# Normalising softmax rows inside the transpose, and two small steps moved to ScalarE

## The chip, the cores and the metric

The kernel runs on one core of a Trainium2 chip. The metric is the device time of one execution in microseconds, as the median of several. The core has five engines with a queue each: TensorE (PE, its weight loads PEld), VectorE (DVE), ScalarE (ACT), GpSimd (POOL) and SyncE (SP), which issues the DMAs. Each takes its own instructions in order.

## The reference

Three layers follow each other: an attention that keeps only the 32 largest scores of each row, a mixture of eight experts with all tokens going to all experts, and a feed-forward layer.

```python
scores = scale * q @ k.T                       # 2 batches, 8 heads, 576 positions, head size 64
kth = np.partition(scores, -32, axis=-1)[..., -32:-31]
scores = np.where(scores >= kth, scores, -1e9)
attn = np.exp(scores - scores.max(-1, keepdims=True))
attn = attn / (attn.sum(-1, keepdims=True) + 1e-9)
x = (attn @ v) as (1152, 512)
P = exp(x @ w_gate - max), 8 rounds of row and column normalisation
x = sum over e of P[:, e] * (relu(x @ w1[e]) @ w2[e])     # 512 -> 1024 -> 512, 8 experts
h = x @ w_in;  out = (h * tanh(softplus(h))) @ w_out      # 512 -> 2048 -> 512
```

## The kernel before

The 1152 tokens are nine tiles of 128. The experts go over them in three chunks: tiles 0 and 1, tiles 2 and 3, tiles 4 to 8. First the attention of tiles 0 and 1 runs alone (16 units, one for each tile and head); then the experts of the first two chunks run on TensorE with the attention of tiles 2 to 8 woven in between, then the third chunk, then the feed-forward layer.

A unit of attention is five stages, and `attention()` writes out by hand in which step each unit's stage is issued: step u issues the scores of unit u, the threshold of unit u-2, the mask of unit u-3, the normalisation of unit u-4 (u-3 from unit 13 on) and the values of unit u-5 (u-4). In the steps from 5 on, two further sets of scores (`early`) are made ahead for later tiles and evicted by ScalarE (L239).

- `scores` (L226, L235): products in PSUM, evicted by ScalarE to `s`, 128x576.
- `threshold` (L254, L261): VectorE finds the 32 largest of each row, by four MAX8 of eight each and three MATCH_REPLACE8 between them.
- `exponential` (L271, L272): `nb` is the row's largest score times -0.125, a 128x1 TENSOR_SCALAR on VectorE, and is the bias of ScalarE's exponential.
- `mask`: for the first 13 units (`on_pool`) VectorE makes a mask (L285), GpSimd adds it to the scores (L286), and ScalarE takes the exponential with the sum `sm` beside it. For the others the exponential is taken first, and VectorE masks and sums in one instruction (L290).
- `norm`: VectorE adds epsilon (L299) and takes the reciprocal (L300), and ScalarE multiplies `em`, 128x576, by it in place (L305).
- `values`: TensorE transposes four blocks of 128x128 (L325) with the identity, ScalarE evicts them (L328); for each pair of heads the last 64 columns of both are one further block (L336, L339). Then the products with v (L348, L355), and for tile 1 the two parts of x (L362, L363).

The order on TensorE is the order in which the program issues its work. On the other engines a planner orders the instructions ahead of time, by the streams that the code names with `st(...)`: "first" goes before "evict", "prep" (the weight copies L520 and L522), "attn", "moe" and "fill". Epsilon and reciprocal of the first 13 units are in the stream "moe", the rest of the attention in "attn". The first MAX8 of tile 2 is tied behind the last reciprocal of tile 1 (`live["ends"]`). Of the small tiles (`top`, `nb`, `sm`, `r`) there are four buffers each. The experts' matmuls are L619 (h, whose two parts are made at L537 and L538) and L596 (y); the first chunk's y are spilled through the two buffers `ysp`.

Of the kernel before, what the change touches and what calls it, by code (L numbers as in the profile page):

```python
# [10 lines left out]
F32 = mybir.dt.float32  # L11
F32R = mybir.dt.float32r
U32 = mybir.dt.uint32
AF = mybir.ActivationFunctionType
ALU = mybir.AluOpType
# [4 lines left out]
P = 128  # L20
B, H, S, D = 2, 8, 576, 64
# [4 lines left out]
DM = H * D  # L26
# [8 lines left out]
TOPK = 32  # L35
NEG = -3.0e38
SCALE = 0.125
EPS = 1e-9
TINY2 = ((1 + 1 / 16) * 2.0**-15) ** 2

CHUNKS = [(0, 1), (2, 3), (4, 5, 6, 7, 8)]
# [32 lines left out]
def attention_moe_moe2(ctx: ExitStack, tc: tile.TileContext, qT, kT, vm, vt, wg, wst, w64, out):  # L74
    nc = tc.nc
# [5 lines left out]
    def after(inst, earlier):  # L81

        tc.add_manual_dep(
            inst.ins,
            earlier.ins.name,
            mybir.DependencyInfo(mybir.DependencyClass.NoSync, mybir.DependencyReason.DATA),
            reason="order",
        )

    def pool(name, bufs=1, space=None, stack=ctx, side="left", **kw):  # L90
        if space is not None:
            kw["space"] = space
        return stack.enter_context(tc.tile_pool(name=name, bufs=bufs, side=side, **kw))

    const = pool("const")
    small = pool("small", 4)
    yp = pool("yp", 2)
# [12 lines left out]
    sp = pool("sp", 2, stack=att)  # L110
    hp = pool("hp", LAG + 1, stack=att)

    with st("attn"):
        ident = const.tile([P, P], F32, name="ident")
# [31 lines left out]
    qset, live, away = {}, {}, {}  # L146
# [14 lines left out]
    def load_v(b, pair):  # L161
        hs = slice(2 * pair, 2 * pair + 2)
        m = vp.tile([P, 2, 4, D], F32, tag="vm", name=f"vm_{b}_{pair}")
        nc.sync.dma_start(m, vm[b, :, hs])
        e = vp.tile([P, P], F32, tag="vt", name=f"vt_{b}_{pair}")
        nc.gpsimd.memset(e, 0.0)
        for i in range(2):
            nc.sync.dma_start(e[i * D : (i + 1) * D, i * D : (i + 1) * D], vt[b, :, 2 * pair + i])
        vmain[b, pair], vtail[b, pair] = m, e
# [22 lines left out]
    def queries(t, g):  # L192
        if (t, g) not in qset:
            qset[t, g] = load_q(t, g)
        return qset[t, g]
# [49 lines left out]
    def threshold(t, h, on_pool):  # L245

        with st("attn"):
            s = live["s", t, h]
            top = small.tile([P, TOPK], F32, tag="top", name=f"top_{t}_{h}")
            w = sp.tile([P, S], F32, tag="w", name=f"w_{t}_{h}")  # L250
            src = s
            for i in range(TOPK // 8):
                g = top[:, 8 * i : 8 * i + 8]
                top8 = nc.vector.max(g, src)  # L254
                if i == 0 and t == CHUNKS[0][-1] + 1:
                    if "ends" in live:
                        after(top8, live["ends"])
                    else:
                        live.setdefault("held", []).append(top8)
                if i + 1 < TOPK // 8:  # L260
                    nc.vector.match_replace(w, g, src, NEG)  # L261
                    src = w
            live["top", t, h] = top
            if not on_pool:
                live["e", t, h] = exponential(t, h, sp.tile([P, S], F32, tag="e", name=f"e_{t}_{h}"), s, nc.vector)
        yield from ()

    def exponential(t, h, dst, src, eng, **kw):

        nb = small.tile([P, 1], F32, tag="nb", name=f"nb_{t}_{h}")  # L270
        eng.tensor_scalar(nb, live["top", t, h][:, 0:1], -SCALE, None, op0=ALU.mult)  # L271
        nc.scalar.activation(dst, src, AF.Exp, bias=nb, scale=SCALE, **kw)  # L272
        return dst

    def mask(t, h, on_pool):

        with st("attn"):
            s = live.pop(("s", t, h))
            sm = small.tile([P, 1], F32, tag="sm", name=f"sm_{t}_{h}")
            kth = live["top", t, h][:, TOPK - 1 : TOPK]  # L280
            if h % 2 == 0:
                live["pair", t, h] = sp.tile([P, 2 * S], F32, tag="em", name=f"em_{t}_{h}", bufs=3)
            em = live["pair", t, h - h % 2][:, h % 2 * S :][:, :S]
            if on_pool:
                nc.vector.tensor_scalar(em, s, kth, NEG, op0=ALU.is_lt, op1=ALU.mult)  # L285
                nc.gpsimd.tensor_tensor(em, em, s, ALU.add)  # L286
                exponential(t, h, em, em, nc.vector, accum_out=sm)
            else:
                e = live.pop(("e", t, h))
                nc.vector.scalar_tensor_tensor(em, s, kth, e, op0=ALU.is_ge, op1=ALU.mult, accum_out=sm)  # L290
            live["em", t, h], live["sm", t, h] = em, sm
        yield from ()

    def norm(t, h, on_pool):
        with st("attn"):
            em, sm = live["em", t, h], live.pop(("sm", t, h))
            r = small.tile([P, 1], F32, tag="r", name=f"r_{t}_{h}")
            with st("moe" if on_pool else "attn"):
                nc.vector.tensor_scalar(r, sm, EPS, None, op0=ALU.add)  # L299
                inv = nc.vector.reciprocal(r, r)  # L300
            if (t, h) == (CHUNKS[0][-1], H - 1):
                live["ends"] = inv
                for inst in live.pop("held", ()):
                    after(inst, inv)
            nc.scalar.activation(em, em, AF.Copy, scale=r)  # L305
        yield from ()

    def turned(t, i, name):

        if t <= CHUNKS[0][-1] and i % 2:  # L310
            bank = ps_m.tile([P, 512], F32, tag="mm2", name=name, bufs=2)
        else:
            bank = ps_a.tile([P, 512], F32, tag="tr", name=name)
        return bank.rearrange("p (c k) -> p c k", k=P)

    def values(t, h):

        if "gate" in live:
            yield from gate_logits(*live.pop("gate"))
        j = h % 2  # L320
        with st("attn"):
            em = live.pop(("em", t, h))
            tr = turned(t, h, f"tr_{t}_{h}")
            for c in range(4):
                nc.tensor.transpose(tr[:, c, :], em[:, j * D + c * P :][:, :P], ident)  # L325
            at = sp.tile([P, 4, P], F32, tag="at", name=f"at_{t}_{h}", bufs=2)
            with st("evict"):
                nc.scalar.activation(at, tr, AF.Copy)  # L328
            live["at", j] = at
        yield  # L330
        if j == 0:
            return
        pair = h // 2
        with st("attn"):
            tr2 = turned(t, 1, f"tr2_{t}_{h}")
            nc.tensor.transpose(tr2[:, 0, :], live.pop(("pair", t, h - 1))[:, 4 * P : 5 * P], ident)  # L336
            at2 = sp.tile([P, P], F32, tag="at2", name=f"at2_{t}_{h}")
            with st("evict"):
                nc.scalar.activation(at2, tr2[:, 0, :], AF.Copy)  # L339
        yield  # L340
        with st("attn"):
            if pair == 0:
                live["pv"] = ps_a.tile([P, NC, P], F32, tag="pv", name=f"pv_{t}")
            pv = live["pv"]
            for b, c0, c1, _, _ in queries(t, h // HG):
                for c in range(4):
                    for i in range(2):
                        nc.tensor.matmul(  # L348
                            pv[i * D : (i + 1) * D, pair, c0:c1],
                            vmain[b, pair][:, i, c, :],  # L350
                            live["at", i][:, c, c0:c1],
                            start=(c == 0),
                            stop=False,
                        )
                nc.tensor.matmul(pv[:, pair, c0:c1], vtail[b, pair], at2[:, c0:c1], start=False, stop=True)  # L355
            if t == 4 and pair + 1 < NC:
                load_v(1, pair + 1)
            ci, i = place[t]
            if t == CHUNKS[0][-1]:
                with st("first"):  # L360
                    hi, lo = (x[:, pair, i * P : (i + 1) * P] for x in x_tiles(ci))
                    nc.scalar.activation(hi, pv[:, pair, :], AF.Copy)  # L362
                    nc.vector.tensor_sub(lo, pv[:, pair, :], hi)  # L363
            elif h == H - 1:
                hi, lo = (x[:, :, i * P : (i + 1) * P] for x in x_tiles(ci))
                nc.scalar.activation(hi, pv, AF.Copy)
                nc.vector.tensor_sub(lo, pv, hi)
            if h == H - 1:
                if t == CHUNKS[ci][-1]:
                    live["gate"] = (ci,)  # L370
                live["done"] = t
        yield
# [487 lines left out]
```

## Time and profile before

| | |
|---|---|
| median of 3 runs | 1221.68 us (1221.15 to 1223.91) |
| the profiled execution | 1221.39 us, span 1219.6 us |
| TensorE busy | 1168.7 us, 96% |
| VectorE busy | 854.7 us, 70% |
| ScalarE busy | 660.2 us, 54% |
| GpSimd busy | 540.8 us, 44% |
| the chain that ended last | PE 86%, DVE 11%, DMA 1%, ACT 1% |

The span is the time from the first to the last instruction in the profile; the execution's own time has about 1.8 us around it. Busy shares are means over all stages, so they are read by windows: a table of the busy time of each engine in a stretch. The chain of waits goes from the last instruction back to whatever released each step. In a timeline, an instruction's duration can reach over the start of the next one on the same engine, so the time that it takes from a full queue is read from start to start. Several equal instructions in a row are one line with a count.

### The profile page before, as it was taken

To read this page: it belongs to the slowest core of one execution; us is meant where nothing else is said; L and a number is where in the kernel's file an instruction comes from. 1 tells how busy PE (TensorE), PEld (TensorE's weight loads), DVE (VectorE), ACT (ScalarE), POOL (GpSimd) and SP (SyncE) were. 2 spreads that over 40 slices of the span, in tenths; PEclk is the share of its full clock that TensorE was granted. 3 is DMA by queue.
4 is the path that set the end of the run, shared out by engine and by line. 5 is a ranking of instruction groups with operands and counts; after the bars stand their busy time and mean duration, and the time that the engine had idled before them with its cause. 6 is when DMAs were issued, how large, how long until landed. Compare 5 with 4: busy or idle time off the path is not lost.

```text
span 1219.6 us, 21194 instructions
## 1 busy us (share of the span) xinstructions
PE 1168.7 (96%) x7459; PEld 1048.4 (86%) x7459; DVE 854.7 (70%) x1873; ACT 660.2 (54%) x1321; POOL 540.8 (44%) x424
## 2 busy tenths in 40 slices
PE   2677999999999999999999999999999999999998
PEld 2566888998989899899999999999999999999997
DVE  7999999999999999713656868677666633433221
ACT  6786777877777778654223333333333334554432
POOL 7844778877777877774112112121121122221210
PEclk9899999999999999999999999999999999999999
DMA  8434565576655555665235665656445332223201
GB/s 258 126 129 152 171 178 170 170 224 188 211 163 168 157 162 164 186 220 169 70 89 180 199 190 176 207 178 192 138 134 160 119 98 64 93 95 114 78 26 44
DMA packets 105114, 183.20 MB, mean 150 GB/s; under 512 B 14128, under 2 KB 24624, under 8 KB 105008
## 3 DMA queue, kind: packets, MB, share of 16 engines
q1 hardware_dynamic: 103712, 180.68, 47.6%
q8 instruction: 58, 0.95, 0.3%
q10 hardware_dynamic: 1296, 1.18, 0.3%
q14 instruction: 48, 0.39, 0.1%
HBM read 158.55 MB, written 23.27 MB: 149 GB/s over the span
## 4 chain that ended last, share of the span: by engine, by line
PE 86%; DVE 11%; DMA 1%; ACT 1%; issue 0%; POOL 0%; SPq 0%; POOLq 0%; ACTq 0%
PE h_c2e L619 18%; PE y_c2e L596 18%; PE h_d L619 8%; PE y_d L596 8%; PE y_c0e L596 7%; PE h_c0e L619 7%; PE h_c1e L619 6%; PE y_c1e L596 6%; DVE top L254 4%; DVE w L261 4%; PE pv L348 2%; PE tr L325 2%; PE sc L226 2%; PE pv L355 1%; DVE em L290 1%; DMA wraw_c0e<-in_wst_dram 1%
## 5 line engine op out<-in xcount | busy, mean ns | idle before, releaser
L522 POOL TENSOR_TENSOR wl_c2e<-wraw_c2e,wh_c2e 128x512 fp32r<-128x512 f32 x64 | 84.2, 1315 | 341.2 <-ACT wh_c2e L520 326.5
L522 POOL TENSOR_TENSOR wl_c0e<-wraw_c0e,wh_c0e 128x512 fp32r<-128x512 f32 x128 | 171.6, 1356 | 53.1 <-ACT wh_c0e L520 50.9
L522 POOL TENSOR_TENSOR wl_c1e<-wraw_c1e,wh_c1e 128x512 fp32r<-128x512 f32 x128 | 173.3, 1371 | 48.6 <-ACT wh_c1e L520 45.2
L520 ACT ACTIVATE wh_c2e<-wraw_c2e 128x512 fp32r<-128x512 f32 x128 | 80.8, 632 | 186.9 <-PE y_c2e L596 95.0
L254 DVE MAX8 top<-w 128x8 f32<-128x576 f32 x216 | 157.8, 747 | 0.8
L619 PE MATMUL h_c2e<-xh,wh_c2e 128*128 128x256 f32 (+1 forms) x512 | 158.3, 309 | 0.0
L619 PE MATMUL h_c2e<-xl,wh_c2e 128*128 128x256 f32 (+1 forms) x512 | 158.0, 309 | 0.0
L619 PE MATMUL h_c2e<-xh,wl_c2e 128*128 128x256 f32 (+1 forms) x512 | 157.8, 308 | 0.0
L538 DVE SCALAR_TENSOR_TENSOR hl_c2e<-h_c2e,hh_c2e 128x256 fp32r<-128x256 f32 (+1 forms) x128 | 62.5, 488 | 99.7 <-ACT hh_c2e L537 99.3
L596 PE MATMUL y_c2e<-wh_c2e,hh_c2e 128*128 128x512 f32 x320 | 126.0, 394 | 0.0
L596 PE MATMUL y_c2e<-wl_c2e,hh_c2e 128*128 128x512 f32 x320 | 125.9, 394 | 0.0
L596 PE MATMUL y_c2e<-wh_c2e,hl_c2e 128*128 128x512 f32 x320 | 125.2, 391 | 0.0
L522 POOL TENSOR_TENSOR wl_d<-wraw_d,wh_d 128x512 fp32r<-128x512 f32 x32 | 41.5, 1297 | 160.2 <-ACT wh_d L520 160.2
L520 ACT ACTIVATE wh_c0e<-wraw_c0e 128x512 fp32r<-128x512 f32 x128 | 80.5, 629 | 52.9 <-PE y_c0e L596 21.0
L261 DVE MATCH_REPLACE8 w<-top,w 128x576 f32<-128x576 f32 x144 | 106.4, 740 | 0.0
L557 DVE TENSOR_TENSOR hl_d<-mg_d,hh_d 128x256 fp32r<-128x256 f32 x64 | 38.5, 602 | 91.7 <-ACT hh_d L556 91.7
L520 ACT ACTIVATE wh_c1e<-wraw_c1e 128x512 fp32r<-128x512 f32 x128 | 80.3, 629 | 40.4 <-PE y_c1e L596 16.4
L619 PEld LDWEIGHTS h_c2e<-xh,wh_c2e 128*128 128x128 f32 x512 | 96.2, 188 | 2.5
L619 PEld LDWEIGHTS h_c2e<-xl,wh_c2e 128*128 128x128 f32 x512 | 96.1, 188 | 2.3
L619 PEld LDWEIGHTS h_c2e<-xh,wl_c2e 128*128 128x128 f32 x512 | 96.8, 189 | 0.0
L226 PE MATMUL sc<-ks,q 128*128 128x288 f32 x320 | 63.1, 330 | 26.0 <-ACT early L239 8.2
L537 ACT ACTIVATE hh_c2e<-h_c2e 128x256 fp32r<-128x256 f32 (+1 forms) x128 | 54.8, 428 | 55.3 <-PE h_c2e L619 53.0
(170 smaller groups left out, 3352.8 us busy)
## 6 DMA issues: line engine op xcount, KB each, us to landing
wraw_c0e<-in_wst_dram SPq DMA_DIRECT2D x128, 256.0 KB, 3.0
wraw_c1e<-in_wst_dram SPq DMA_DIRECT2D x128, 256.0 KB, 3.0
wraw_c2e<-in_wst_dram SPq DMA_DIRECT2D x128, 256.0 KB, 3.0
cx<-in_w_dram SPq DMA_DIRECT2D x32, 512.0 KB, 4.2
wraw_d<-w SPq DMA_DIRECT2D x64, 256.0 KB, 2.6
yd<-ysp SPq DMA_DIRECT2D x32, 256.0 KB, 3.6
yb<-yd SPq DMA_DIRECT2D x32, 256.0 KB, 3.2
w<-cc SPq DMA_DIRECT2D x32, 256.0 KB, 3.5
```

The lines of the kernel that those rows point to most:

```text
L226: nc.tensor.matmul(halves[half], q[:, h % HG, :], ks[b, h][:, half * HS : (half + 1) * HS], start=(i == 0), stop=(i == len(terms) - 1),)
L254: top8 = nc.vector.max(g, src)
L261: nc.vector.match_replace(w, g, src, NEG)
L325: nc.tensor.transpose(tr[:, c, :], em[:, j * D + c * P :][:, :P], ident)
L348: nc.tensor.matmul(pv[i * D : (i + 1) * D, pair, c0:c1], vmain[b, pair][:, i, c, :], live["at", i][:, c, c0:c1], start=(c == 0), stop=False,)
L520: nc.scalar.activation(hi, raw, AF.Copy)
L522: eng.tensor_sub(lo, raw, hi)
L537: nc.scalar.activation(h, ps, AF.Relu)
L538: live["hl"] = nc.vector.scalar_tensor_tensor(l, ps, 0.0, h, op0=ALU.max, op1=ALU.subtract)
L557: nc.vector.tensor_sub(l, g, h)
L596: nc.tensor.matmul(y, h[:, j * P : (j + 1) * P], w, start=(f == 0 and k == 0), stop=(f == nf - 1 and k == 2),)
L619: nc.tensor.matmul(ps, w[:, c * P : (c + 1) * P], x[:, c, c0 : c0 + m], start=(k == 0), stop=(k == 3 * NC - 1),)
```

## The change

For tiles 0 and 1 the exponentials are no longer scaled in place. ScalarE multiplies the identity (128x128) by the reciprocals instead, which gives a diagonal, and TensorE multiplies each block of exponentials by it, where it transposed with the identity. The output is the transposed and scaled block. The last block of a pair, which holds 64 columns of either head, becomes two matmuls with 64 columns each, one for each head's diagonal. The diagonals of a pair lie in a tile of `ysp`. Also for tiles 0 and 1, `nb` is made by ScalarE, and for the first 13 units epsilon is added by ScalarE. `top`, `nb` and `sm` get six buffers.

```diff
-            top = small.tile([P, TOPK], F32, tag="top", name=f"top_{t}_{h}")
+            top = small.tile([P, TOPK], F32, tag="top", name=f"top_{t}_{h}", bufs=6)
...
-        nb = small.tile([P, 1], F32, tag="nb", name=f"nb_{t}_{h}")
-        eng.tensor_scalar(nb, live["top", t, h][:, 0:1], -SCALE, None, op0=ALU.mult)
+        nb = small.tile([P, 1], F32, tag="nb", name=f"nb_{t}_{h}", bufs=6)
+        top = live["top", t, h][:, 0:1]
+        if t <= CHUNKS[0][-1]:
+            nc.scalar.activation(nb, top, AF.Copy, scale=-SCALE)
+        else:
+            nc.vector.tensor_scalar(nb, top, -SCALE, None, op0=ALU.mult)
         nc.scalar.activation(dst, src, AF.Exp, bias=nb, scale=SCALE, **kw)
...
-            sm = small.tile([P, 1], F32, tag="sm", name=f"sm_{t}_{h}")
+            sm = small.tile([P, 1], F32, tag="sm", name=f"sm_{t}_{h}", bufs=6)
...
             with st("moe" if on_pool else "attn"):
-                nc.vector.tensor_scalar(r, sm, EPS, None, op0=ALU.add)
+                if on_pool:
+                    nc.scalar.activation(r, sm, AF.Copy, bias=EPS)
+                else:
+                    nc.vector.tensor_scalar(r, sm, EPS, None, op0=ALU.add)
                 inv = nc.vector.reciprocal(r, r)
...
-            nc.scalar.activation(em, em, AF.Copy, scale=r)
+            if t > CHUNKS[0][-1]:
+                nc.scalar.activation(em, em, AF.Copy, scale=r)
+            else:
+                if h % 2 == 0:
+                    live["turn", t, h] = yp.tile([P, DM], F32, tag="ysp", name=f"turn_{t}_{h}")
+                turn = live["turn", t, h - h % 2][:, h % 2 * P :][:, :P]
+                nc.scalar.activation(turn, ident, AF.Copy, scale=r)
...
             for c in range(4):
-                nc.tensor.transpose(tr[:, c, :], em[:, j * D + c * P :][:, :P], ident)
+                part = em[:, j * D + c * P :][:, :P]
+                if t > CHUNKS[0][-1]:
+                    nc.tensor.transpose(tr[:, c, :], part, ident)
+                else:
+                    nc.tensor.matmul(tr[:, c, :], part, live["turn", t, h - j][:, j * P :][:, :P], start=True, stop=True)
...
-            nc.tensor.transpose(tr2[:, 0, :], live.pop(("pair", t, h - 1))[:, 4 * P : 5 * P], ident)
+            tail = live.pop(("pair", t, h - 1))[:, 4 * P : 5 * P]
+            if t > CHUNKS[0][-1]:
+                nc.tensor.transpose(tr2[:, 0, :], tail, ident)
+            else:
+                turn = live.pop(("turn", t, h - 1))
+                for i in range(2):
+                    keys = slice(i * D, (i + 1) * D)
+                    nc.tensor.matmul(tr2[keys, 0, :], tail[:, keys], turn[:, i * P :][:, :P], start=True, stop=True)
```

## Rows read from the trace of the kernel before

**Rows 1.** Windows: busy us of PE, PEld, DVE, ACT, POOL; clock, DMA share, GB/s.

```profile
33.00:104.50 71.50, 51.29 (x321) 40.81 (x321) 71.43 (x181) 58.58 (x136) 41.66 (x34) 0.90 0.45 144
...
108.20:122.20 14.00, 11.93 (x80) 10.44 (x79) 14.00 (x34) 8.76 (x18) 8.81 (x7) 1.00 0.32 94
122.20:1219.60 1097.40, 1092.90 (x7005) 987.70 (x7005) 741.32 (x1599) 570.19 (x1128) 465.44 (x351) 1.00 0.48 148
```

**Rows 2.** Chain that ended last, 95 to 125 us: start, us, what.

```profile
104.47 0.16 DVE r L300
...
121.89 0.33 DVE hl_c0e L538
...
122.27 1.65 PE h_c0e L619 x12
```

**Rows 3.** Groups, VectorE, 0 to 104.5 us: count, busy us, mean ns, idle before.

```profile
L285 DVE TENSOR_SCALAR em<-s,top 128x576 f32<-128x576 f32 x13 | 10.9, 842 | 0.0
...
L299 DVE TENSOR_SCALAR r<-sm 128x1 f32<-128x1 f32 x16 | 2.2, 140 | 0.0
L271 DVE TENSOR_SCALAR nb<-top 128x1 f32<-128x1 f32 x16 | 2.2, 143 | 1.2 <-ACT em L272 1.2
```

**Rows 4.** Timeline, VectorE, 10 to 62 us: start us, us, operation, count, idle before.

```profile
17.57 0.76 DVE L254 MAX8 top<-s 128x8 f32<-128x576 f32 x1 [0.50 <-ACT s L235]
...
25.62 0.15 DVE L271 TENSOR_SCALAR nb<-top 128x1 f32<-128x1 f32 x1 [0.85 <-ACT em L272]
...
25.75 0.80 DVE L285 TENSOR_SCALAR em<-s,top 128x576 f32<-128x576 f32 x1
...
38.27 0.74 DVE L254 MAX8 top<-s 128x8 f32<-128x576 f32 x1
...
44.51 0.74 DVE L261 MATCH_REPLACE8 w<-top,s 128x576 f32<-128x576 f32 x1
...
48.61 1.72 DVE L285 TENSOR_SCALAR em<-s,top 128x576 f32<-128x576 f32 x1
...
55.39 0.50 DVE L285 TENSOR_SCALAR em<-s,top 128x576 f32<-128x576 f32 x1
...
57.26 0.14 DVE L299 TENSOR_SCALAR r<-sm 128x1 f32<-128x1 f32 x1
57.32 0.07 DVE L261 MATCH_VALUE_LOAD w<-top,w 128x8 f32 x1
```

**Rows 5.** Timeline, ScalarE, 20 to 105 us.

```profile
25.40 0.19 ACT L272 ACTIVATION_READ_ACCUMULATOR em<-em,nb 128x1 f32 x1
25.49 1.13 ACT L520 ACTIVATE wh_c0e<-wraw_c0e 128x512 fp32r<-128x512 f32 x2
...
97.36 0.76 ACT L305 ACTIVATE em<-em,r 128x576 f32<-128x576 f32 x1
98.02 0.25 ACT L362 ACTIVATE xh<-pv 128x128 fp32r<-128x128 f32 x1
98.18 0.71 ACT L239 ACTIVATE early<-sc 128x288 f32<-128x288 f32 x2
```

**Rows 6.** Timeline, TensorE, 20 to 77 us.

```profile
30.05 1.12 PE L325 MATMUL tr<-ident,em 128*128 128x128 f32 x4 [8.44 <-ACT em L305]
...
73.82 0.60 PE L325 MATMUL tr<-ident,em 128*128 128x128 f32 x4
74.25 0.27 PE L336 MATMUL tr<-ident,em 128*128 128x128 f32 x1
...
75.21 1.09 PE L348 MATMUL pv<-at,vm 128*64 128x128 f32 x14 [0.32 <-ACT at L328]
76.23 0.49 PE L355 MATMUL pv<-at,vt 128*128 128x128 f32 x2
76.47 0.78 PE L226 MATMUL sc<-ks,q 128*128 128x288 f32 x4
```

**Rows 7.** Waits to 130 us: waiter, awaited, us in total, times, longest.

```profile
PE tr L325 <- ACT em L305: 15.0, 6, 8.4
```

More of the change, by code (lines that the diff above doesn't have):

```diff
@@ L264, in threshold, with exponential @@
             if not on_pool:
-                live["e", t, h] = exponential(t, h, sp.tile([P, S], F32, tag="e", name=f"e_{t}_{h}"), s, nc.vector)
+                live["e", t, h] = exponential(t, h, sp.tile([P, S], F32, tag="e", name=f"e_{t}_{h}"), s)
         yield from ()
-    def exponential(t, h, dst, src, eng, **kw):
-        nb = small.tile([P, 1], F32, tag="nb", name=f"nb_{t}_{h}")
-        eng.tensor_scalar(nb, live["top", t, h][:, 0:1], -SCALE, None, op0=ALU.mult)
+    def exponential(t, h, dst, src, **kw):
+        nb = small.tile([P, 1], F32, tag="nb", name=f"nb_{t}_{h}", bufs=6)
[4 more added lines that the diff above has]
+            nc.vector.tensor_scalar(nb, top, -SCALE, None, op0=ALU.mult)
         nc.scalar.activation(dst, src, AF.Exp, bias=nb, scale=SCALE, **kw)
@@ L286, in mask @@
                 nc.gpsimd.tensor_tensor(em, em, s, ALU.add)
-                exponential(t, h, em, em, nc.vector, accum_out=sm)
+                exponential(t, h, em, em, accum_out=sm)
             else:
```

## The prediction

> **What bounds the kernel now.** I read the windows first. The program is two stretches. From 122.2 us to the end TensorE is busy 1092.9 of 1097.4 us [rows 1]: it has no idle time to give back, and the change adds and removes nothing there. What can move is the moment at which this stretch begins. In 33.0 to 104.5 us VectorE is busy 71.43 of 71.50 us, while TensorE has 51.3 and ScalarE 58.6 of it [rows 1]. The chain of waits says the same: back from 122.27, where TensorE's unbroken work starts, it stays on VectorE, by the h pieces' low part at 121.89 and by the reciprocal at 104.47 [rows 2]. That reciprocal is the last of tiles 0 and 1. Tile 2's first MAX8 is ordered behind it, so VectorE's work up to it is a fixed set: less work there ends the first phase sooner, by as much, if VectorE stays without gaps. TensorE waits 15.0 us on the scaling of em up to 130 us [rows 7], mostly early (8.44 us in one piece at 30.05, rows 6), but VectorE had other units to work on meanwhile, so this wait is not what sets the end.
>
> **The change part by part.**
>
> *VectorE loses 29 small instructions.* 16 bias products (L271) and 13 of the 16 additions of epsilon (L299; units 13 to 15 keep theirs) [rows 3]. Each lasts 0.14 us, but the next instruction starts 0.06 us later (57.26 to 57.32, rows 4); in a full queue the spacing is the price. VectorE waits for scores for the last time at 17.57 [rows 4]; the bias products of units 0 to 2 lie about there or before and give nothing. So 26 x 0.06 = 1.6 us; bounds 1.6 and, by the durations, 29 x 0.14 = 4.1. I take 1.6, since the queue's spacing was seen directly.
>
> *Two stalls in front of L271.* It waited 1.2 us in all for ScalarE's exponential [rows 3], 0.85 us of it at 25.62 [rows 4]: a bias buffer (4 of them) is free only when the exponential four units back has read it. Off VectorE and with 6 buffers that wait is not VectorE's. The next thing in its queue but the epsilon, which also leaves, is the mask at 25.75 [rows 4], which needs neither. I take the whole 1.2; the other end is 0, if the reciprocal, which still needs the sum, is put in the same place and waits there instead.
>
> *The mask L285.* 13 of them take 10.9 us, 0.84 on average [rows 3], between 0.50 (at 55.39) and 1.72 (at 48.61) [rows 4]; 13 x 0.50 would be 6.5. The 4.4 us over that depend on what else runs beside each, and the new order will deal them out anew. I take 0, with 2 us to either side.
>
> *ScalarE: scaling 128x576 becomes 128x128.* The old one takes 0.66 us of the queue (97.36 to 98.02), the nearest 128x128 row 0.16 (98.02 to 98.18) [rows 5]: 16 x 0.50 = 8.0 us less. Added are 29 one-column activations. The nearest row is the accumulator read, 0.19 long with the next start 0.09 later [rows 5]; so 2.6 to 5.5 us more, and I take 0.09, the queue's spacing. Net 5.4 us less (2.5 at least), on an engine that is not the bound. [...]
>
> *New waits on ScalarE.* Each bias product now waits there for the unit's first MAX8. Queued behind it are exponentials, evictions of scores (L235) and of transposes (L328); TensorE and VectorE's next MAX8 wait for these. With 5.4 us less work on it, and idle 12.9 of 71.5 us, I cost this at nothing; without that cover each microsecond by which VectorE is behind ScalarE's order would be lost to evictions. The epsilon follows its exponential on the same engine, at the lowest of the orders in use there (the stream "moe"); see the rivals. The reciprocal no longer sits behind an epsilon on VectorE.
>
> *TensorE: transposes become fp32 matmuls.* Four transposes take 0.43 us of the queue (73.82 to 74.25). A matmul of the same shape, L355, is two records and takes 0.24 (76.23 to 76.47) [rows 6]; four of them 0.96, so 0.53 us more for each unit, 8.5 us for 16. The pair's tail was one transpose, 0.11 at a quarter of 0.43; it becomes two half-width matmuls, four records at 0.073 (75.21 to 76.23 for 14), 0.29: 0.2 more, 1.5 us for 8. That is 10 us at full clock. At 30.05 four transposes span 1.12 us instead of 0.60 [rows 6]; where it is so, the surplus may be double, too. TensorE has 20.2 us idle in 33.0 to 104.5 alone [rows 1], so this lies beside VectorE's work. The rows of L325 and L355 differ by 2.2 times. [...]
>
> *The end of the phase.* After the last reciprocal: scaling, four transposes, eviction, products, first h piece. The scaling gets 0.50 shorter, the transposes 0.53 longer; the tail lies beside the eviction. I take 0, from -0.5 to +0.9.
>
> *Buffers.* top, nb and sm with 6 buffers, and the diagonal in ysp's two buffers, which nothing else uses before the first y is spilled, cost no time of their own.
>
> Sum: 1.6 + 1.2 = 2.8 us less. The profiled execution took 1221.39 us (span 1219.6 and 1.8 around it): 1218.6. The median of before is 0.3 above that execution, so 1218.9 for the median.
>
> **The rivals.**
>
> *The loop gets shorter as well.* With epsilon beside its exponential, the reciprocal has one VectorE slot to wait for instead of two, diagonals and so TensorE's evictions come sooner, and fewer masks are stretched. For it: TensorE's 15.0 us of waiting on em [rows 7], the 4.4 us over in L285. Against: VectorE has no idle time to fill after 33 us. If half of the 4.4 and 1 us of the end are added: 1218.9 - 3.2 = 1215.7.
>
> *The saving is taken back.* Reciprocals are now the place where VectorE waits for ScalarE, which is busy 82% of the phase [rows 1]. If the 1.2 us stay and the slots (1.6) go into such waits or into masks stretched again: 1221.7, no change. The same holds if the time saved before 104.47 is lost among the MAX8s of tile 2, beside which VectorE is busy 14.0 of 14.0 us up to 122.2 [rows 1]. Against: before, the epsilon waited for the same exponential, and after 33 us VectorE stood still for none of them.
>
> *Slower: the epsilon comes late.* A unit's scores are issued on TensorE behind the transposes of an earlier unit, so whatever delays the diagonal delays scores. On ScalarE the epsilon has the lowest order: after the first exponential weight copies follow at once (25.49, rows 5), and in the phase ScalarE is busy 82% of the time. VectorE's reserve is about 6.2 us: unit 6's scores are first read at 38.27 and its first replacement starts only at 44.51 [rows 4], older units filling the time. From 6.2 us of delay in sum VectorE idles, and each further microsecond is lost. An epsilon later by 1 us than VectorE's was, in each of 13 units, gives 13 - 6.2 = 6.8 lost, less the 2.8 gained: 1225.7. Against: ScalarE has 12.9 us of gaps in the phase, one for nearly each epsilon, and on VectorE the epsilon and the reciprocal each had to find a slot in a full queue.
>
> [...]
>
> **How the numbers follow.** A measurement of this kernel tells about 0.2% (2.4 us) from no change, so faster is below 1219.2. Forecast, 1217 to 1220.5: 0.47, of which 0.33 lies below 1219.2. Shorter loop, 1213 to 1217: 0.15. Taken back, 1220.5 to 1224: 0.19. Slower, above 1224: 0.19 (0.13 by a late epsilon, 0.06 by dearer matmuls). Faster 0.48, same 0.33, slower 0.19. The range of 8 in 10 leaves out the lower half of the second case and the upper two thirds of the last: 1214.5 to 1225.0.
>
> **What would show it.** Right: no idle time before L271's successors on VectorE near 25 us, the last reciprocal of tile 1 some 2.8 us earlier than 104.47, TensorE's unbroken work from about 119.5, and the same 1097 us behind it. [...] Wrong: waits of reciprocals on ScalarE, of MAX8 on scores, masks that add up to far from 10.9 us, or TensorE waiting in the stretch behind.

## The result, and the profile after

The changed kernel takes 1230.57 us (median of 4 runs, 1229.88 to 1232.17) beside 1222.8 us of the kernel before in the same runs: 1.0066 times as long, 95% interval 1.0046 to 1.0085. It is slower by about 8 us where 2.8 us less were forecast, and it lies outside the range. The profiled execution took 1232.17 us, its span 1230.2; against the profiled execution of before the span is 10.6 us longer.

Lines moved by the change: the mask is now L289, the reciprocal L307, the diagonal L318, the transposing matmuls L342 and L360, eviction of transposes L345, products L372 and L379, the parts of x L386 and L387, y L620 and h L643.

Windows of after: busy us of PE, PEld, DVE, ACT, POOL; clock, DMA share, GB/s. They answer to [rows 1]; the middle one runs from the last reciprocal of tile 1 to the first h piece.

```profile
33.00:104.50 71.50, 52.69 (x365) 46.06 (x366) 67.84 (x151) 54.77 (x153) 41.69 (x34) 0.86 0.44 139
107.03:110.84 3.81, 3.34 (x34) 2.61 (x33) 3.81 (x8) 1.65 (x4) 0.00 (x0) 1.00 0.18 67
110.80:1230.20 1119.40, 1112.85 (x7085) 999.79 (x7084) 759.75 (x1634) 579.92 (x1145) 471.74 (x357) 1.00 0.47 147
```

The same last stretch of before, which also starts with its first h piece:

```profile
108.20:1219.60 1111.40, 1104.83 (x7085) 998.14 (x7084) 755.32 (x1631) 578.96 (x1145) 474.26 (x357) 1.00 0.47 148
```

Two things are to be seen. First, VectorE is no longer full in the first phase: 67.84 busy of 71.50 where it had 71.43 [rows 1]. Second, and larger: after the first h piece TensorE runs the same 7085 matmuls at the same granted clock, 1.00, and is busy 8.0 us longer (1112.85 against 1104.83). Its idle time is the same 6.6 us in both. So the matmuls themselves have become slower, in a stretch which the change does not touch.

The chain of waits of after (start, us, what), for [rows 2]:

```profile
106.51 0.29 ACT xh L386
106.82 0.29 DVE xl L387
107.11 0.07 DVE r L307
107.19 3.94 DVE top L254 x6
```

The last reciprocal of tile 1 starts at 107.03 instead of 104.47, so the first phase is 2.6 us longer, not 2.8 shorter. The other 8.0 us of the 10.6 are the slower matmuls.

Groups of VectorE in after, 0 to 107.1 us (count, busy us, mean ns, idle before and what ended it), for [rows 3]:

```profile
L254 DVE MAX8 top<-s 128x8 f32<-128x576 f32 x16 | 12.0, 752 | 6.1 <-ACT s L235 6.0
L289 DVE TENSOR_SCALAR em<-s,top 128x576 f32<-128x576 f32 x13 | 9.3, 715 | 0.0
L307 DVE RECIPROCAL r<-r 128x1 f32<-128x1 f32 x16 | 2.4, 151 | 0.6 <-ACT r L304 0.6
L387 DVE TENSOR_TENSOR xl<-pv,xh 128x128 fp32r<-128x128 f32 x3 | 0.9, 288 | 2.3 <-ACT xh L386 2.3
```

And its timeline (start us, us, operation, count, idle before), for [rows 4]:

```profile
23.42 0.76 DVE L254 MAX8 top<-s 128x8 f32<-128x576 f32 x1 [1.71 <-ACT s L235]
...
25.48 0.15 DVE L307 RECIPROCAL r<-r 128x1 f32<-128x1 f32 x1
25.55 0.92 DVE L289 TENSOR_SCALAR em<-s,top 128x576 f32<-128x576 f32 x1
...
106.82 0.29 DVE L387 TENSOR_TENSOR xl<-pv,xh 128x128 fp32r<-128x128 f32 x1 [1.05 <-ACT xh L386]
107.03 0.15 DVE L307 RECIPROCAL r<-r 128x1 f32<-128x1 f32 x1
107.10 1.40 DVE L254 MAX8 top<-early 128x8 f32<-128x576 f32 x2
108.42 2.72 DVE L254 MAX8 top<-early_xh 128x8 f32<-128x576 f32 x4
```

The stall before the bias product (0.85 us at 25.62, rows 4) is gone, but two microseconds earlier the first MAX8 of a unit stands 1.71 us for its scores. At the end the last reciprocal, which has its inputs, is queued behind a low part of x that waits 1.05 us for ScalarE. Behind it six MAX8 of tile 2 run at once, where there were four.

### The profile page after: what moved, and what is told of

The parts are those of the page before. It is cut to its first block, busy times and chain, and to the rows that moved or that the text cites. A ratio compares the mean times of both kernels' runs of the same rounds, so it can differ in the third digit from the quotient of the medians.

```text
span 1230.2 us, 21361 instructions
## 1 busy us (share of the span) xinstructions
PE 1183.8 (96%) x7547; PEld 1060.1 (86%) x7547; DVE 856.8 (70%) x1844; ACT 658.8 (54%) x1350; POOL 538.4 (44%) x424
## 4 chain that ended last, share of the span: by engine, by line
PE 92%; ACT 3%; POOL 2%; DMA 2%; DVE 1%; issue 1%; POOLq 0%; ACTq 0%
PE y_c2e L620 18%; PE h_c2e L643 18%; PE h_d L643 8%; PE y_d L620 8%; PE y_c1e L620 7%; PE h_c0e L643 7%; PE h_c1e L643 7%; PE y_c0e L620 7%; PE pv L372 3%; PE sc L226 2%; PE tr L340 2%; PE pv L379 1%; DMA kraw<-in_kT_dram 1%; PE tr L342 1%; POOL ks L158 1%
## 5 line engine op out<-in xcount | busy, mean ns | idle before, releaser
L546 POOL TENSOR_TENSOR wl_c1e<-wraw_c1e,wh_c1e 128x512 fp32r<-128x512 f32 x128 | 169.9, 1343 | 57.1 <-ACT wh_c1e L544 56.6
L643 PE MATMUL h_c2e<-xh,wl_c2e 128*128 128x256 f32 (+1 forms) x512 | 157.9, 308 | 0.0
L643 PE MATMUL h_c2e<-xh,wh_c2e 128*128 128x256 f32 (+1 forms) x512 | 157.7, 308 | 0.0
L643 PE MATMUL h_c2e<-xl,wh_c2e 128*128 128x256 f32 (+1 forms) x512 | 157.4, 307 | 0.0
L620 PE MATMUL y_c2e<-wh_c2e,hh_c2e 128*128 128x512 f32 x320 | 127.0, 397 | 0.0
L620 PE MATMUL y_c2e<-wh_c2e,hl_c2e 128*128 128x512 f32 x320 | 126.6, 396 | 0.0
L620 PE MATMUL y_c2e<-wl_c2e,hh_c2e 128*128 128x512 f32 x320 | 126.6, 396 | 0.0
L643 PEld LDWEIGHTS h_c2e<-xl,wh_c2e 128*128 128x128 f32 x512 | 96.2, 188 | 2.8
L643 PEld LDWEIGHTS h_c2e<-xh,wh_c2e 128*128 128x128 f32 x512 | 96.0, 188 | 2.5
L643 PEld LDWEIGHTS h_c2e<-xh,wl_c2e 128*128 128x128 f32 x512 | 96.1, 188 | 0.0
```

The lines of the kernel that those rows point to most:

```text
L546: eng.tensor_sub(lo, raw, hi)
L620: nc.tensor.matmul(y, h[:, j * P : (j + 1) * P], w, start=(f == 0 and k == 0), stop=(f == nf - 1 and k == 2),)
L643: nc.tensor.matmul(ps, w[:, c * P : (c + 1) * P], x[:, c, c0 : c0 + m], start=(k == 0), stop=(k == 3 * NC - 1),)
```

## What slows the matmuls: the place of the tiles

TensorE's timeline shows the slower matmuls one by one. In the third chunk a y block is 15 matmuls of 512 columns without a gap; it is read from its first start to the start of the h that follows. Before:

```profile
842.23 0.39 PE L596 MATMUL y_c2e<-wh_c2e,hh_c2e 128*128 128x512 f32 x1
...
845.45 0.39 PE L596 MATMUL y_c2e<-wh_c2e,hl_c2e 128*128 128x512 f32 x1
845.67 0.28 PE L619 MATMUL h_c2e<-xh,wh_c2e 128*128 128x256 f32 x1
```

After:

```profile
851.01 0.39 PE L620 MATMUL y_c2e<-wh_c2e,hh_c2e 128*128 128x512 f32 x1
...
854.27 0.40 PE L620 MATMUL y_c2e<-wh_c2e,hl_c2e 128*128 128x512 f32 x1
854.50 0.28 PE L643 MATMUL h_c2e<-xh,wh_c2e 128*128 128x256 f32 x1
```

3.44 us against 3.49, 229 against 233 ns for each matmul. What the change did to them: `top`, `nb` and `sm` stand in one of the first pools from the left side of SBUF. Two more buffers of each are 2 x 128 + 2 x 32 + 2 x 32 = 384 bytes in every partition, and every left-side tile behind them moves by as much: x and the h pieces, which TensorE reads. The weights of the experts lie in a pool on the right side and stay. In 256 bytes, x and the h pieces stood at 128 and the weights at 192, 64 apart; after the change x and h stand at 0, 192 apart.

The first theory was that this move, and nothing else, costs the 8 us. The rival was that the changed work of tiles 0 and 1 costs it, by what it leaves behind for tile 2 and later. An empty tile of so many bytes beside the small ones moves everything behind it and changes no instruction and no engine's order:

```diff
-    small = pool("small", 4)
+    small = pool("small", 4); pool("pad").tile([P, 96], F32, name="pad")
```

**Before, all moved by 384 bytes** (the edit above in the kernel before).

> The kernel before, with 384 unused bytes in each partition behind the small tiles, as many as the six buffers of top, nb and sm take more in the changed kernel. Everything allocated on that side behind them (x, h, k, em, the diagonals' tile) stands 384 bytes further; the weights, allocated from the other side, don't move; every engine's order is that of before. Theory 'addresses' (the 8 us that the changed kernel loses after its first h piece come from where the tiles lie): about 1230 us, first h piece at 108.3 as before, but the y matmuls of c2e spaced by some 234 ns instead of 230.5 and the h matmuls of c0e by 117.4 instead of 115.9. Rival 'later work' (they come from the shifted order and arrival of work): 1222 us, spacings as before.

Measured: 1229.47 us, ratio 1.008 [1.0058, 1.0102]. The kernel before becomes as slow as the changed one, with none of its instructions changed.

**The change, moved back to a whole 512 bytes** (in the changed kernel a pad of [P, 32], so 384 + 128).

> The changed kernel, with 128 unused bytes behind the small tiles: all tiles behind them now stand 512 bytes from their places in the kernel before, instead of 384. Every engine's order is that of the changed kernel. Theory 'addresses', with a pattern that repeats at 512 bytes: the spacings of before (y of c2e 230.5 ns), first h piece at 110.8, and 1222.8 + 2.6 = 1225.4 us. Rival 'later work': 1230.6 us, as the changed kernel. If addresses matter but not with a period of 512 bytes, spacings are neither's.

Measured: 1225.24 us, ratio 1.0029 [1.0011, 1.0047]; its ten runs spread from 1219.64 to 1227.45, wider than any other here, and the profiled one was near the low end (span 1217.9). About five of the 8 us are gone at the median. The matmuls are as fast as before's in the profile; the first h piece, expected at 110.8, came at 107.8 there. The rest of this section and the next come back to what is left.

**Before, moved by 256 bytes** ([P, 64]).

> The kernel before with 256 unused bytes behind the small tiles instead of 384; orders as before. Asks what of the address matters. Theory 'distance to the weights in 512 bytes': x and h stand at 384 in a line of 512 where the weights stand at 448, before at 128, with 384 bytes more at 0. If any shift but 512 costs, 1229 as with 384; if nearness to 0 does, 1220 to 1222; spacings of c0e's h between 115.9 and 117.4 ns show which.

Measured: 1219.74 us, 0.9995 [0.9984, 1.0006]. No cost.

**Before, moved by 128 bytes** ([P, 32]).

> The kernel before with 128 unused bytes: x and h at 256 in a line of 512; orders as before. Theory 'addresses, period 256': as slow as with 384 bytes (at 0), 1229, h matmuls of c0e spaced by 117.4 ns and y matmuls of c2e by 234. Rival 'period 512': as before, 1220, 115.9 and 230.

Measured: 1228.56 us, 1.0064 [1.0047, 1.008]. As slow as 384, where 256 cost nothing: so far the pattern repeats every 256 bytes.

**The change, moved to 768 bytes** (changed kernel, [P, 96]).

> The changed kernel with 384 unused bytes behind its small tiles: tiles behind them 768 bytes from their places in the kernel before, at 384 in a line of 512; orders those of the changed kernel. Theory 'addresses': another place that isn't the changed kernel's 0 gives the spacings of before, and a median like that of the changed kernel moved by 128, 1225.2, or less. Its executions should again fall apart by TensorE's granted clock, 1220 at 0.997 and 1226 at 0.991 to 0.993, if the first phase of the changed order hangs on that clock; a profile that falls low shows the first h piece near 110.8, one that falls high near 107.8. Rival 'the order alone': 1225 to 1226 whatever the clock.

Measured: 1222.56 us, 1.0009 [0.9998, 1.0019]. Back beside the kernel before. The ten executions did not fall apart by the granted clock, as was expected: one at 0.997 took 1222.83 us, one at 0.994 1219.98.

What matters could be where x and h stand, or how far they stand from the weights. The next two runs move the weights instead, by 128 bytes, and leave every left-side tile where it was:

```diff
-    pool("edge", side="right").tile([P, 8], F32, name="edge")
+    pool("edge", side="right").tile([P, 40], F32, name="edge")
```

**The change, weights moved.**

> The changed kernel with 128 more unused bytes at the other end, so that the weights' tiles, and nothing else, stand 128 bytes lower; x and h stay at 0 in a line of 256. Orders those of the changed kernel. Theory 'distance' (x, h and the weights that TensorE reads one beside the other cost more at some distances in 256 bytes): the distance is that of the kernel before again, the spacings of before (h of c0e 115.9, y of c2e 230 ns), 1222 to 1226 us. Theory 'own place': x and h at a multiple of 256 are slow wherever the weights are, 117.4 and 234 ns, 1230 us.

Measured: 1221.18 us, 1.0006 [0.9989, 1.0023]. In its TensorE timeline a y block takes 3.44 us again:

```profile
841.73 0.39 PE L620 MATMUL y_c2e<-wh_c2e,hh_c2e 128*128 128x512 f32 x1
...
845.17 0.28 PE L643 MATMUL h_c2e<-xh,wh_c2e 128*128 128x256 f32 x1
```

**Before, weights moved.**

> The kernel before with only the weights' tiles 128 bytes lower; orders as before. Theory 'distance': the distance is now that of the changed kernel, so 117.4 and 234 ns and 1229 us, though x and h stand where they did. Theory 'own place': 115.9 and 230 ns, 1220 us.

Measured: 1228.97 us, 1.0069 [1.005, 1.0089]. So the same x, at the same address, is fast or slow by the place of the weights: the theory that x's own place decides falls; at these places the distance decides.

**Before, moved by 64 and by 192 bytes** ([P, 16] and [P, 48]), the two distances that were left. The question was whether a short distance is the bad thing, or one value is good by luck.

> The kernel before with 64 unused bytes behind the small tiles; orders as before. x and h stand at 192 in a line of 256, as the weights do: distance 0. If the changed kernel's distance is the odd one, 1220 us and 115.9 and 230 ns; if 64 is a lucky one, 1229 or more; if a distance of 0 is better still, h of c0e under 115.5 ns and under 1219 us.

> The kernel before with 192 unused bytes; orders as before. x and h stand at 64 in a line of 256, distance 128 to the weights. Between the two measured ones: if the cost goes with the distance, about 1224 us and 116.5 ns; if only the changed kernel's distance costs, 1220 us.

Measured: 1228.89 us, 1.007 [1.0042, 1.0098], and 1233.87 us, 1.0113 [1.0089, 1.0137]. Both are slow, so of the four distances only 64 is good; for the second, neither of the two forecasts, 1224 and 1220, came. Windows from the first h piece to the end, first of the run moved by 384 bytes, then of the changed kernel with the weights moved, then of before moved by 192 (columns as above):

```profile
108.42:1226.70 1118.28, 1113.61 (x7085) 1000.80 (x7084) 754.21 (x1628) 579.74 (x1144) 472.24 (x357) 1.00 0.47 147
```

```profile
109.39:1218.20 1108.81, 1102.13 (x7085) 995.26 (x7084) 757.92 (x1634) 578.22 (x1145) 473.60 (x357) 1.00 0.48 148
```

```profile
108.85:1232.60 1123.75, 1117.53 (x7085) 1007.05 (x7084) 755.29 (x1631) 580.80 (x1145) 471.19 (x357) 1.00 0.47 146
```

The same 7085 matmuls at granted clock 1.00 take TensorE 1102 to 1118 us. By distance, weights less x and h, in 256 bytes (last three columns: mean ns from the start of one matmul to the start of the next with the same output and width, from all of their records, without intervals over one and a half times the median):

| distance | runs | median us | first h to end | h, chunk 1, 256 columns | y, chunk 3 | y, last layer |
|---|---|---|---|---|---|---|
| 64 | before as it is or moved 256; the change, moved 512, 768 or with weights moved | 1219.7 to 1225.2 | 1108.8 to 1111.6 | 115.6 to 115.8 | 230.0 to 230.5 | 229.7 to 229.8 |
| 0 | before, moved 64 | 1228.9 | 1118.2 | 119.1 | 230.5 | 229.8 |
| 192 | after; before, moved 384, 128 or with weights moved | 1228.6 to 1230.6 | 1118.3 to 1119.7 | 117.3 to 117.7 | 233.9 to 234.0 | 229.2 to 229.6 |
| 128 | before, moved 192 | 1233.9 | 1123.8 | 119.0 | 233.3 | 229.9 |

The four runs at 192 agree in y to 0.03 ns (233.93 to 233.96), with two kernels and three ways to get there. The last layer has both cases side by side. Its second weights stand on the left side beside what they meet and move with it, and its y hardly changes. Its first weights stand on the right, and its h of 256 columns takes 116.9 to 117.1 ns at 64, 117.4 to 117.8 at 192, 119.5 at 0 and 119.9 at 128. In the chunks of the table, h is about 1.5% slower at 192 and y 1.6%, at 0 h 2.9% and y 0.2% at most, at 128 h 2.8% and y 1.3%; three of four distances cost 7 to 12 us beside before in the same runs, and the kernel before stood at the fourth. Why the hardware does so, no run here shows.

## What the change itself is worth

Seven more kernels stand at the good distance, 64; their results tell what the rest of the change does. From the first h to the end they take 1107.9 to 1113.4 us. A ratio is to the kernel before in the same runs.

**The buffers alone** (before, with six buffers of the three tiles and a pad of 128 bytes).

```diff
-    small = pool("small", 4)
+    small = pool("small", 4); pool("pad").tile([P, 32], F32, name="pad")
...
-            top = small.tile([P, TOPK], F32, tag="top", name=f"top_{t}_{h}")
+            top = small.tile([P, TOPK], F32, tag="top", name=f"top_{t}_{h}", bufs=6)
...
-        nb = small.tile([P, 1], F32, tag="nb", name=f"nb_{t}_{h}")
+        nb = small.tile([P, 1], F32, tag="nb", name=f"nb_{t}_{h}", bufs=6)
...
-            sm = small.tile([P, 1], F32, tag="sm", name=f"sm_{t}_{h}")
+            sm = small.tile([P, 1], F32, tag="sm", name=f"sm_{t}_{h}", bufs=6)
```

> The kernel before with six buffers of top, nb and sm and nothing else of the change; 128 unused bytes behind them, so that the tiles behind stand 512 bytes from their old places. Theory 'six MAX8' (six buffers of top let six MAX8 of tile 2 run ahead at the end of the first phase, where four did, and the low parts of x wait behind them): 2 to 3.5 us slower than before, 1222.5 to 1223.5 beside 1220, six MAX8 in a row behind the last reciprocal. Rival 'buffers are free': within 0.1% of before.

Measured: 1219.58 us, 0.9998 [0.9985, 1.001]. With their bytes made harmless, the buffers cost nothing. The six MAX8 in a row did not come: the low part of x was set behind the third.

**The steps moved to ScalarE alone**: the edit above, and of the change only `nb` and epsilon:

```diff
+        if t <= CHUNKS[0][-1]:
+            nc.scalar.activation(nb, top, AF.Copy, scale=-SCALE)
...
+                if on_pool:
+                    nc.scalar.activation(r, sm, AF.Copy, bias=EPS)
```

> Of the change only the bias products and the additions of epsilon on ScalarE, with six buffers of top, nb and sm; em is scaled in place and transposed as before. 128 unused bytes as in the run beside it. Theory 'matmuls' (TensorE's diagonal matmuls, made longer by its lower clock in the first phase, delay scores and x by more than VectorE saves): the last reciprocal of tile 1 comes 2 to 3 us earlier than 104.47, and the time is 1220 us. Rival 'ScalarE' (the small instructions on ScalarE delay evictions): last reciprocal at 106 to 107, 1225 us.

Measured: 1223.97 us, 1.0034 [1.0019, 1.0049]. The last reciprocal comes at 103.06, 1.4 us earlier than before, but the first h piece only at 110.65. VectorE's timeline, and TensorE's under it:

```profile
103.06 0.16 DVE L307 RECIPROCAL r<-r 128x1 f32<-128x1 f32 x1
103.14 1.40 DVE L254 MAX8 top<-early 128x8 f32<-128x576 f32 x2
104.46 2.72 DVE L254 MAX8 top<-early_xh 128x8 f32<-128x576 f32 x4
...
107.88 0.28 DVE L370 TENSOR_TENSOR xl<-pv,xh 128x128 fp32r<-128x128 f32 x1
```

```profile
108.30 1.97 PE L355 MATMUL pv<-at,vm 128*64 128x128 f32 x16 [2.96 <-DVE xl L370]
```

Six MAX8 of tile 2, two more than before because `top` has six buffers, are set ahead of the low part of x, and TensorE stands 2.96 us for that. What the moves gain is lost here; the time lies nearer to the rival's 1225 than to the 1220 of the theory.

**The diagonals alone**: buffers and pad as above, and of the change only the part with `turn`, on both engines:

```diff
+                nc.scalar.activation(turn, ident, AF.Copy, scale=r)
...
+                    nc.tensor.matmul(tr[:, c, :], part, live["turn", t, h - j][:, j * P :][:, :P], start=True, stop=True)
```

> Of the change only the diagonals, with six buffers of top, nb and sm; bias products and epsilon stay on VectorE. 128 unused bytes as in the runs beside it. Theory 'matmuls': the last reciprocal later than in the changed kernel's 107.0 or about there, VectorE idle by 3 to 5 us more than before, half-clock stretches about 20 us in the first phase, and 1225 to 1227 us. Rival 'ScalarE': 104 to 104.5, 1222 us.

Measured: 1223.07 us, 1.0029 [1.0017, 1.004]; the last reciprocal comes at 105.4, the first h at 111.1, and TensorE waits 1.17 us for the low part of x. The time lies between the two forecasts.

Then the same with `top` at four buffers, the other two tiles at six, and a pad of 384 bytes that makes the move a whole 512:

```diff
-            top = small.tile([P, TOPK], F32, tag="top", name=f"top_{t}_{h}", bufs=6)
+            top = small.tile([P, TOPK], F32, tag="top", name=f"top_{t}_{h}")
```

**The whole change**, so:

> The changed kernel with four buffers of top instead of six (nb and sm keep six), and 384 unused bytes, so that the tiles behind stand 512 bytes from their places in the kernel before. Theory 'six MAX8': about 2 us faster than the same with six, so 1222 to 1223 us where that had 1225.2; what is left over before is TensorE's longer first phase. Rival: 1225.

Measured: 1218.72 us, 0.9985 [0.9975, 0.9996]. Four MAX8 follow the last reciprocal, and it comes at 103.91:

```profile
103.70 0.29 DVE L387 TENSOR_TENSOR xl<-pv,xh 128x128 fp32r<-128x128 f32 x1 [0.18 <-ACT xh L386]
103.91 0.15 DVE L307 RECIPROCAL r<-r 128x1 f32<-128x1 f32 x1
103.98 1.40 DVE L254 MAX8 top<-early 128x8 f32<-128x576 f32 x2
105.30 1.40 DVE L254 MAX8 top<-early_xh 128x8 f32<-128x576 f32 x2
```

1222 to 1223 were expected. It is the only version whose interval lies below 1, by 0.15%, less than the 0.2% that were called no change.

**The moves, so:**

> Only the bias products and epsilons on ScalarE, nb and sm with six buffers, top with four, em scaled in place and transposed as before; tiles 512 bytes from their old places. Theory 'six MAX8' with theory 'matmuls': last reciprocal at about 103 as with six buffers (103.06), first h piece at 106.5 to 107 instead of 110.7, and 1218 to 1219 us, 1 to 2 us faster than before. Rival: 1222 to 1224, as with six.

Measured: 1219.41 us, 0.9997 [0.9984, 1.0011]; last reciprocal 103.4, first h 107.2, both earlier than before's, in the profiled execution by 1.0 us.

**The diagonals, so:**

> Only the diagonals, with four buffers of top, six of nb and sm; bias products and epsilons on VectorE, tiles 512 bytes from their old places. With six buffers of top it took 1223.1. Theory 'six buffers': 1219 to 1220.5; VectorE's last reciprocal near 105. Rival 'TensorE's matmuls': 1222 to 1223, first h piece at 110 or later.

Measured: 1222.03 us, 1.0017 [1.0003, 1.0031]; last reciprocal 105.0, first h 109.4. The rival's time came, not the 1219 to 1220.5 of the theory.

**The whole change with four buffers of all three**, without a pad: every tile is where it was before.

> The changed kernel with four buffers of top, nb and sm, as before the change; every tile at its old place. Theory 'six buffers': 1218.5 to 1220, no slower than before, so that the buffers are what makes the change slow, by the addresses that they move and by the order that six buffers of top bring. Rival 'TensorE': 1222 to 1225, since the matmuls, the clock and the new waits are all there.

Measured: 1220.45 us, 0.9997 [0.9987, 1.0008]. The plain answer to what diagonals and moves are worth, nothing else touched: nothing.

So neither part brings anything that can be measured, and what either costs goes with the order that the planner gives it: with six `top` buffers instead of four the moves stand at 1.0034 instead of 0.9997 and the diagonals at 1.0029 instead of 1.0017, while six buffers alone cost nothing. The whole change stands at 1.0029, 1.0009 and 1.0006 with six, at 0.9985 and 0.9997 with four.

In the profiled executions of the changed order the first phase also goes with TensorE's granted clock. The windows 33.0 to 104.5 us of three executions in which every engine has the order of the changed kernel: moved back to 512, weights moved, moved to 768:

```profile
33.00:104.50 71.50, 52.60 (x391) 45.26 (x390) 68.78 (x157) 55.14 (x154) 41.15 (x33) 0.95 0.47 146
```

```profile
33.00:104.50 71.50, 53.35 (x381) 45.73 (x380) 70.41 (x158) 54.71 (x152) 41.34 (x33) 0.88 0.45 142
```

```profile
33.00:104.50 71.50, 52.60 (x352) 45.74 (x352) 67.61 (x151) 53.56 (x149) 40.49 (x33) 0.83 0.43 132
```

With the granted clock at 0.95, 0.88, 0.86 (after) and 0.83 in the mean, the first h starts at 107.8, 109.4, 110.8 and 112.4 us. The seven profiled executions in the order of before show less of it: 107.0 at 0.93, 108.1 to 108.9 in four at 0.90, 108.2 and 108.9 in two at 0.88. In the traces of before and after the granted clock has only two levels, 1.00 and 0.50, so a mean below 1 is time at 0.50, and the timeline of after shows one such piece:

```profile
91.39 1.05 PE L342 MATMUL tr<-turn,em 128*128 128x128 f32 x8
92.20 0.77 PE L226 MATMUL sc<-ks,q 128*128 128x288 f32 x4
94.94 0.83 PE L226 MATMUL sc<-ks,q 128*128 128x288 f32 x4 [1.97 <-ACT early L239]
95.61 1.71 PE L342 MATMUL tr<-turn,em 128*128 128x128 f32 x8
97.25 0.70 PE L360 MATMUL tr<-turn,em 128*64 128x128 f32 x4
```

TensorE stood 1.97 us for ScalarE, the granted clock was 0.50 soon after it went on (96.0 to 99.0), and the eight diagonal matmuls at 95.61 took 1.64 us from start to start. The run moved back to 512 has the same order and the same wait, and there the granted clock stayed at 1.00 (92.5 to 96.5):

```profile
92.54 0.83 PE L226 MATMUL sc<-ks,q 128*128 128x288 f32 x4 [1.96 <-ACT early L239]
93.22 1.05 PE L342 MATMUL tr<-turn,em 128*128 128x128 f32 x8
94.20 0.44 PE L360 MATMUL tr<-turn,em 128*64 128x128 f32 x4
```

Here they took 0.98. The lower level, 0.50, goes with 0.66 us more at this one place, and the wait alone did not bring it. That the clock moves the end of the phase, and not both something else, was not tried; four executions in one order stand for it. Whole executions are mixed: of the ten moved back to 512 the two fastest, 1219.64 and 1219.94, had the highest clocks, 0.998 and 0.997, but the ten moved to 768 do not sort by it.

## Why the prediction was wrong, point by point

**The step that failed** is "Buffers": that six buffers "cost no time of their own". They were priced as buffers, by who waits for one, and there the runs agree (0.9998 for the buffers alone). Their 384 bytes were not priced at all: they set x and h at another distance from the weights, and TensorE's 7085 matmuls behind the first phase took 8.0 us more. With it fell the last sign of being right, "the same 1097 us behind it": the premise that a stretch which the change leaves alone keeps its time. No rival held this; the 0.06 given to dearer matmuls had the right engine and sign, but for the new matmuls of tiles 0 and 1 only.

**VectorE loses 29 instructions; stalls at L271.** They went as said: 29 instructions less, which gave 1.8 us of the queue for 1.6 forecast, and no stall near 25.6. The masks L289 even came down to 9.3 us from 10.9 [rows 3], on the good side of the 2 us allowed; that is chance, as they took 9.2 to 10.9 in the four executions of this order. What runs beside a mask showed in its length: in before the six with at most 0.3 us of GpSimd's work beside them took 0.50 to 0.51 us, the other seven 0.70 to 1.72. But the sum asked for VectorE to stay without gaps, and it did not. From start to start up to the last reciprocal all its slots are 2.4 us less and its idle time 5.0 us more (13.8 against 8.8), 2.6 us net, which is the 107.03 for 104.47. The new idle time is for scores (1.71 at 23.42, 0.91 at 76.1), for the low part of x (1.20 and 1.05) and for an epsilon (0.61). So the second step that failed is "New waits on ScalarE", costed at nothing in the cover of ScalarE's 12.9 idle us. This is the rival "taken back", with its waits on ScalarE; of reciprocals it is the smallest part. Scores stood among the signs of being wrong, without a price; the low part of x stood nowhere. How large the loss is differs by execution: in the four of this order the last reciprocal came at 104.0, 105.6, 107.0 and 108.6, in the seven of before's order at 103.2 to 105.1, and in none at the 101.7 that the forecast asks for. The run with four buffers agrees with "taken back": 1220.45, where 1221.7 was forecast for it.

**ScalarE, net 5.4 us less.** Busy in 33.0 to 104.5: 3.8 us less. The one-column copies are right, the diagonal is not. ScalarE's timeline in after:

```profile
48.53 0.24 ACT L273 ACTIVATE nb<-top 128x1 f32<-128x1 f32 x1
48.63 0.45 ACT L239 ACTIVATE early_xh<-sc 128x288 f32<-128x288 f32 x1
...
50.72 0.40 ACT L318 ACTIVATE turn<-ident,r 128x128 f32<-128x128 f32 x1 [0.23 <-DVE r L307]
51.05 0.65 ACT L235 ACTIVATE s<-sc 128x576 f32<-128x576 f32 x1
```

`nb` takes 0.10 of the queue (0.09 forecast), the diagonal 0.33 here and 0.29 in most places (0.16 forecast, read from an eviction of PSUM, rows 5). At 0.29, 16 x 0.13 = 2.1 us of the 5.4 were not there. What the eviction lacked can be estimated from rows. From 128 to 576 columns a copy scaled by a tile grows from 0.29 to 0.66 (L305, rows 5), so one of 512 would take 0.61; a plain one from SBUF took 0.52 (L186, 88.93 to 89.45 in before) and one from PSUM 0.48 (L328, 91.46 to 91.94). So some 0.09 go with the tile of scales and 0.04 with SBUF. For one column a full queue has 0.10 us on ScalarE (48.53 to 48.63) against 0.06 on VectorE [rows 4], and no run has the diagonal on VectorE.

**TensorE, 10 us in the cover of its idle time.** At a granted clock of 1.00 a unit's four blocks take 0.98 from start to start where the pair's tail follows, for 0.96 forecast; four transposes took 0.43 in such a place [rows 6]. Where scores follow, the blocks take 0.81 (91.39 to 92.20) and four transposes took 0.36. Before:

```profile
78.94 0.60 PE L325 MATMUL tr<-ident,em 128*128 128x128 f32 x4
79.30 0.84 PE L226 MATMUL sc<-ks,q 128*128 128x288 f32 x4
```

After:

```profile
85.76 1.05 PE L342 MATMUL tr<-turn,em 128*128 128x128 f32 x8
86.74 0.44 PE L360 MATMUL tr<-turn,em 128*64 128x128 f32 x4
```

The end of the phase came as said, too: 107.03 to 110.84 is 3.81 us, and 104.47 to 108.25 was 3.78, so 0.0 for the 0.0 forecast. The blocks take 2.3 times as long as four transposes: 0.98 against 0.43, or 0.81 against 0.36. Where the granted clock was 0.57 in the mean the eight took 1.64 (95.61 to 97.25), 1.7 times the 0.98, so the surplus did grow as the prediction allowed; its own row for that, at 30.05, had a granted clock of 1.00. Whether this or the waits on ScalarE made the phase longer in the profiled execution, no run separates.

**Two slower cases.** A late epsilon: one wait of 0.61 us of a reciprocal, not the 6.8 us lost. Dearer matmuls, the 0.06 among the chances: no run shows them, and at a granted clock of 1.00 four blocks took 0.98 us where L355's spacing gives 0.96.

**Left open:** why the distance matters; why ten executions of the change moved by 512 spread over 8 us; and the third chunk, which takes 445.0 us in before's profile and in two others (steps only, four buffers) and 441.9 to 442.1 in the other nine at that distance. The difference lies in matmuls again, with the same order on TensorE: in chunk 3 those of h with 384 columns follow each other by 175.6 ns in the three and by 173.1 to 173.2 in the nine. So the distance is not all that moves the spacing, and the 8.0 us of after are measured against one of the three. One wait of TensorE of 1.3 us, a transpose for an eviction at 353 us, came with the order in after and with several others, the buffers alone among them; TensorE's idle time behind the first phase is 6.6 us in after as in before all the same.

## What to carry to other kernels

A change that adds or drops a few bytes in SBUF moves tiles that it does not name (here 384 bytes, and TensorE's untouched matmuls took 8.0 us more); where TensorE is the bound, compare the mean spacing of untouched matmuls in both traces first, and keep the old addresses with a pad or with the old number of buffers before judging the change itself. Run the old kernel with the same bytes as an empty tile: here it told in one run, 1229.47 us, whether contents or place made the difference. And the saving on the full engine counted only as far as what feeds it had time to spare: scores and the parts of x from ScalarE became the next waits (1.71 and 1.05 us).

## What the runs showed of the hardware

The distance, in 256 bytes of a partition, between the two operands of a matmul changed how closely matmuls followed each other, at the same granted clock of 1.00: 230.0 to 234.0 ns for 512 columns (y, chunk 3), 115.6 to 119.1 ns for 256 (h, chunk 1), and 1219.7 to 1233.9 us for the kernel before, with no instruction changed. A 128x128 copy from SBUF, scaled by a tile, took 0.29 us of ScalarE's queue in most places, where an eviction of the same size from PSUM took 0.16.
